# Chunked attention and a two-layer network on one core: first transfers halved, float64 weights decoded with a slope, a gate with one ScalarE pass less, and another issue order

## The chip, the cores and the metric

The kernel runs on one core of a Trainium2 chip. The metric is device time in microseconds of one execution. In the text, PE is TensorE, ACT is ScalarE, DVE is VectorE, and SP is the engine whose queue issues the transfers.

## The reference, cut to what matters

Attention over chunks of 32 queries, each with a window of 64 keys (8 memory keys, 16 left, 32 own, 8 right), and then two matrix products with a piecewise square between them. The two weights of the network come as float64.

```
scores = scale * q_c @ k_full.T                # per chunk: 32 x 64, 4 x 8 heads, 24 chunks
a = exp(scores - max) ; a = a / (sum(a) + 1e-9)
x = a @ v_full                                  # x: 3072 tokens x 512
h = x @ w_in                                    # 512 -> 2048
g = h if h >= 1, 0 if h <= -1, else (h + 1)**2 / 4
out = g @ w_out                                 # 2048 -> 512
```

## The kernel before, in words

The 3072 tokens are six blocks of 512. Each product of the network is made of three products of fp32r parts (high by high, low by high, high by low), so every operand is split on ACT (a copy to fp32r: the high part) and DVE (the difference: the low part). The 2048 hidden features are 16 slices of 128 (`NFC`). For one block and one slice, PE does the first layer (12 matmuls into a bank of `ps_h`, of which there are two), ACT and DVE make the gate from that bank, and PE does the second layer (12 matmuls into the accumulators `a0`, `a1`).

The weights arrive as 16 tiles `w_0` to `w_15` of 1 MB, each with two slices of 128 by 512 float64 in the order of `weight_order`: w_0 holds first-layer slices 0 and 1, w_1 first-layer slice 2 and second-layer slice 0, w_2 first-layer slice 3 and second-layer slice 1, and so on. `decode` makes fp32 words of them: ACT scales the upper words by 2^-112 to move the exponent, DVE shifts the upper word left by 3, ors in the top bits of the lower word, ors in the sign bit, ACT copies the high part, DVE subtracts for the low part.

After the first two blocks the work goes on in a fixed main loop, 64 steps of one block and slice. The first two blocks are the string `FIRST`: an order written out by hand, each name standing for the next piece of one chain of work. Every engine keeps the program order (`InOrder`), so the string sets the queue of each engine:

- `g0` to `g3`: attention of block 0, by halves of the block and of the head pairs (`first_attention`). PE scores, DVE maximum and subtraction, ACT exponential, DVE sum, reciprocal and product, PE transposes, ACT copy `pt`, PE values into `ps_x`, ACT copy `xth`, DVE difference `xtl`. g0 and g1 are tokens 0 to 255, g2 and g3 tokens 256 to 511.
- `w0` to `w15`: `decode` of one tile.
- `A0` to `A3` and `B0` to `B3`: block 0, slices 0 to 3, with the first half of the tokens (A) and the second (B). `J4` to `J15`: slices 4 to 15 with all tokens. Pieces of each: first layer, gate on ACT, gate on DVE, high part, low part, second layer (`early_step`). `C`, `D`, `E`: the same for block 1.
- `n0` to `n3`: attention of blocks 1 and 2. `+`: the next transfer of the list `early`.

A0 to A3 need g0 and g1 complete, B0 to B3 need g2 and g3. In the gate, ACT makes `relu(h/2 + 1/2)`, `relu(h - 1)` and the square of the first, and DVE makes `min(square, 1) + relu(h - 1)`; `ps_h` is free when the second relu is done. All eight banks are taken: two of `ps_h`, and two each under the tags `s`, `a0` and `a1`, where scores and values of `g` and `n` also live. In the main loop `gating(s)` and `gate_sum(s - 1)` do the same.

Of the kernel before, what the change touches and what calls it, by code (L numbers as in the profile page):

```python
# [31 lines left out]
FIRST = """  # L32
    + + g0 g0 + g0 g1 g0 + g0 g1 g1 g0 g0 + g1 g0 w0 g1 g0 + g1 g1 g1 g0 w0 g1 + w0 g2 g1 w0 g1 g2 +
    w0 g2 w1 g0 w0 + g2 w1 g1 g2 + g0 g2 g2 g2 + g0 g2 w1 g3 g2 g1 w1 + A0 w2 g3 w1 g3 A1 w2 + g3 w1
    w3 g3 g2 A0 g3 g3 + A1 g3 A2 w2 g2 w4 g3 g2 A2 A0 w2 g3 A0 + g3 w3 w2 A0 w3 A0 g3 g3 + w2 B0 A1
    w3 A3 A1 B0 + A1 w3 B0 B1 w4 B0 w3 A3 A1 + B1 B0 w4 w5 B2 B1 w6 A2 w4 n0 + A2 B1 A2 w4 B1 A2 A3
    w5 A3 B2 + A3 w5 B3 w8 B2 w7 B0 w4 + B2 w5 B3 A3 w9 B2 B3 B1 w6 B3 + w5 w6 J4 w10 B3 w5 + w6 w11
    B2 w7 J4 w7 J5 + w6 w7 w12 w6 + w7 B3 J4 J5 w8 J6 w7 + J4 J5 w13 J4 w9 J5 J4 J6 w9 + J5 w15 J6
    w9 J7 J6 w14 J6 n0 w9 J5 J7 w9 w8 J7 J8 w8 J7 J7 w8 w11 J6 w8 J8 w11 J8 J9 w10 J8 w10 w11 J7 J9
    J8 w10 w11 J9 n0 w10 J10 J9 w10 n0 J9 w12 J8 J10 w12 w12 J11 J10 w12 w11 J10 J10 w13 J9 J11 w12  # L40
    w13 w14 J12 J11 n0 J11 n0 n0 J10 n0 J12 J11 n0 n0 J13 n0 n0 n0 n0 J11 w13 J13 J12 w13 J13 w14
    J12 n0 J13 w13 J12 J14 + n0 w14 n0 n0 w14 J12 w14 J14 J13 J14 w15 J14 n1 w15 w15 J15 + n1 w15
    w15 J13 J15 n1 J15 n1 J14 C0 J15 n1 J14 n1 n1 C0 n1 n1 J15 C1 n1 n1 J15 n1 C1 n1 n1 C1 C0 C1 C2
    J15 J15 C0 C1 n1 J15 J15 C0 C2 C2 C0 + n1 C2 n1 n1 C3 C2 C1 C3 C3 D0 C3 C3 C2 D0 D0 D1 D0 D0 n2
    D1 D1 D2 D1 + n2 C3 D1 D2 n2 D0 D2 n2 D2 D3 n2 D2 D1 n2 n2 D3 n2 E4 D3 n2 D3 n2 n2 n2 D2 E4 D3
    n2 E5 n2 E4 E4 E4 D3 E5 E6 E5 E5 E5 E4 E6 E6 E6 n2 E6 E7 + n2 n2 n2 E7 n3 E5 + n2 n2 E7 E8 E7 n2
    E7 n2 E6 n2 E8 n2 n3 E8 E9 E8 n3 E8 E7 n3 E9 n3 E9 n3 n3 n3 E10 E9 E9 E8 E10 n3 n3 E10 n3 E11
    E10 E10 n3 E9 E11 n3 n3 E11 E12 E11 E11 E10 n3 + E12 n3 E12 n3 n3 E13 E12 E12 n3 E11 E13 n3 n3
    E13 E14 E13 E13 n3 E12 n3 E14 n3 E14 E15 E14 E14 E13 E15 E15 E15 E15
"""  # L50
# [18 lines left out]
def attn_ffn_kernel(ctx: ExitStack, tc: tile.TileContext, first_qk, first_v, qk, vw, w, out):  # L69
# [32 lines left out]

    def load_first_qk(g):

        if g == 0:
            t = apool.tile([P, 2, 2 * QKN], F32, name="qk0", tag="qk")
            qk_of[0, 0], qk_of[0, 1] = t[:, 0], t[:, 1]
        elif g > 1:
            qk_of[0, g] = const.tile([P, 2 * QKN], F32, name=f"qk0_{g}", tag=f"w_{NPW - 5 + g}")
        sp.dma_start(qk_of[0, g], first_qk[g])  # L110

    def load_first_v(g):
        if g % 2 == 0:
            if g == 0:
# [3 lines left out]
            v_of[0, g], v_of[0, g + 1] = t[:, 0], t[:, 1]  # L118
        sp.dma_start(v_of[0, g], first_v[g])
# [23 lines left out]

    def words(i):
        pairs = raw[i].rearrange("p (n two) -> p n two", two=2)
        return pairs[:, :, 0], pairs[:, :, 1]

    def decode(i):

        low, u = words(i)  # L150
        high = u.bitcast(F32)

        act.activation(high, high, AF.Copy, scale=2.0**-112)
        yield
        f = apool.tile([P, n2], U32, name="f", bufs=2)
# [7 lines left out]
        ws[i] = const.tile([P, 2 * n2], F32R, name=f"wr_{i}", tag=f"w_{i}")  # L163
        hi, lo = ws[i][:, 0:n2], ws[i][:, n2 : 2 * n2]
        act.copy(hi, f)
        yield
        dve.tensor_tensor(lo, f, hi.bitcast(F32), op=ALU.subtract)
        yield
# [44 lines left out]
    def first_attention(g):  # L213
# [264 lines left out]
    def gating(s):  # L478

        h = hidden.pop(s)  # L480
        g = gpool.tile([P, TB], F32, name="gw", tag="gw")
        t = gpool.tile([P, TB], F32, name="gt")
        act.activation(g, h, AF.Relu, bias=0.5, scale=0.5)
        act.activation(t, h, AF.Relu, bias=-1.0)
# [30 lines left out]
    def early_step(name, blk, tokens, fc):  # L515
# [25 lines left out]
        g, t, gh, gl = (x[:, n * HT : n * HT + size] for x in tiles)
# [4 lines left out]
        dve.scalar_tensor_tensor(g, g, 1.0, t, op0=ALU.min, op1=ALU.add)  # L546
        yield
# [38 lines left out]
    def keep_warm(n):  # L586
# [5 lines left out]

    early = [
        (load_first_qk, 0), (load_first_qk, 1), (load_first_v, 0), (load_w, 0), (load_first_v, 1),
        (load_first_qk, 2), (load_w, 1), (load_first_qk, 3), (load_first_v, 2), (load_first_v, 3),
        (load_w, 2), (load_w, 3), (load_w, 4), (load_qk, 1, 0), (load_v, 1, 0),
    ]
    early += [(load_w, i) for i in range(5, NPW)]
    early += [(load, blk, half) for blk, half in ((1, 1), (2, 0), (2, 1), (3, 0)) for load in (load_qk, load_v)]
    early = iter(early)  # L600

# [7 lines left out]
        "n": lambda i: attention((1 + i // 2, i % 2)),  # L609
        "w": decode,  # L610
    }
    parts = {"A": (0, (0, 1)), "B": (0, (2, 3)), "J": (0, range(NT))}
    parts |= {"C": (1, (0, 1)), "D": (1, (2, 3)), "E": (1, range(NT))}
    chains = {}
    for name in FIRST.split():
        if name == "+":
            load, *which = next(early)
            load(*which)
            continue
        if name not in chains:  # L620
# [15 lines left out]
    for s in range(first * NFC, steps):  # L636
# [40 lines left out]
    gate_sum(steps - 1)  # L677
    gate_high(steps - 1)
# [94 lines left out]
```

## Time and profile before

| | |
|---|---|
| median of 3 runs | 595.48 us (595.32 to 595.52) |
| the profiled execution | 595.43 us, of which the span from first to last instruction is 593.7 us |
| mean granted clock of TensorE | 0.985 of full |
| busy share: PE, PEld, DVE, ACT | 97%, 81%, 60%, 49% |
| read from and written to memory | 48.23 MB, 6.29 MB |

The profile's page is one execution. A busy PE can be a PE at half its clock, and matmul ends are modelled. Idle time of an engine costs only where the engine bounds its stretch, so the rows are read by stage: the first 35 us, where the clock falls and PE waits, the stretch to 110 us, and the main loop behind it.

### The profile page before, as it was taken

How to read it: one execution, taken by the hardware profiler on the slowest of the kernel's cores; microseconds unless marked ns; L12 is line 12 of the kernel's file. 1: busy time of each engine (PE TensorE's matmuls, PEld its weight loads, DVE VectorE, ACT ScalarE, POOL GpSimd, SP SyncE). 2: the span in 40 equal slices, each digit the busy share in tenths (PEclk: the TensorE clock that was granted, in tenths of full speed). 3: DMA queues.
4: the chain of work that ended last, by engine and by line, in shares of the span. 5: the costliest groups of instructions: out<-in, count | busy, mean ns of one | idle time of the engine just before them, and what ended most of it. 6: DMA issues, size and time to landing. Idle time of an engine off the chain costs nothing.

```text
span 593.7 us, 12316 instructions
## 1 busy us (share of the span) xinstructions
PE 577.6 (97%) x5496; PEld 478.1 (81%) x5496; DVE 357.6 (60%) x506; ACT 288.9 (49%) x511; POOL 0.7 (0%) x6
## 2 busy tenths in 40 slices
PE   5899999999999999999999999999999999999996
PEld 2788888798888888888888888888888888888885
DVE  5999999986576434756723674833584752322222
ACT  2689864545454444444535353444443453543342
POOL 0000000000000000000000000000000000000000
PEclk8599999999999999999999999999999999999999
DMA  8999300425050203113201223201320000100001
GB/s 353 424 416 421 161 0 1 175 75 182 0 179 1 72 1 139 42 71 108 72 1 72 108 72 108 72 1 39 140 72 2 1 2 0 72 0 2 0 1 71
DMA packets 9845, 55.32 MB, mean 93 GB/s; under 512 B 1088, under 2 KB 1088, under 8 KB 5184
## 3 DMA queue, kind: packets, MB, share of 16 engines
q1 hardware_dynamic: 9792, 54.53, 24.0%
q8 instruction: 43, 0.70, 0.5%
q14 instruction: 10, 0.08, 0.0%
HBM read 48.23 MB, written 6.29 MB: 92 GB/s over the span
## 4 chain that ended last, share of the span: by engine, by line
PE 81%; DVE 15%; issue 2%; DMA 1%; ACT 0%; DVEq 0%; ACTq 0%
PE ps_o L63 39%; PE ps_h L63 38%; DVE f L63 6%; DVE wr L63 2%; PE ps_s L63 2%; PE ps_x L63 2%; DVE gw L63 1%; DVE gl L63 1%; DVE pr L63 1%; DVE den L63 1%; DMA qk<-in_first_qk_dram 1%; DVE pt L63 1%; DVE mx L63 1%; DVE xtl L63 0%; DVE rin L63 0%
## 5 line engine op out<-in xcount | busy, mean ns | idle before, releaser
L63 PE MATMUL ps_h<-xth,wr 128*128 128x512 f32 (+1 forms) x832 | 195.4, 377 | 1.0 <-DVE wr L63 1.0
L63 PE MATMUL ps_o<-wr,gh 128*128 128x512 f32 x768 | 194.6, 390 | 0.0
L63 PEld LDWEIGHTS ps_h<-xth,wr 128*128 128x128 f32 x832 | 148.7, 190 | 30.6 <-DVE wr L63 1.5
L63 PEld LDWEIGHTS ps_o<-wr,gh 128*128 128x128 f32 x768 | 143.3, 188 | 29.4
L63 DVE SCALAR_TENSOR_TENSOR gw<-gw,gt 128x512 f32<-128x512 f32 (+1 forms) x104 | 67.2, 648 | 139.3 <-ACT gw L63 138.8
L63 ACT ACTIVATE gw<-ps_h 128x512 f32<-128x512 f32 (+1 forms) x104 | 58.5, 562 | 152.5 <-PE ps_h L63 152.5
L63 PE MATMUL ps_o<-wr,gl 128*128 128x512 f32 x384 | 106.9, 389 | 0.0
L63 PE MATMUL ps_h<-xtl,wr 128*128 128x512 f32 (+1 forms) x416 | 104.8, 374 | 0.0
L63 ACT CAST gh<-gw 128x512 fp32r<-128x512 f32 (+1 forms) x104 | 60.9, 587 | 72.8 <-DVE gw L63 72.8
L63 DVE TENSOR_TENSOR gl<-gw,gh 128x512 fp32r<-128x512 f32 (+1 forms) x104 | 67.3, 648 | 45.7 <-ACT gh L63 45.5
L63 PEld LDWEIGHTS ps_h<-xtl,wr 128*128 128x128 f32 x416 | 75.3, 190 | 13.9
L63 PEld LDWEIGHTS ps_o<-wr,gl 128*128 128x128 f32 x384 | 72.1, 188 | 15.1
L63 ACT ACTIVATE gw<-gw 128x512 f32<-128x512 f32 (+1 forms) x104 | 62.3, 599 | 0.0
L63 ACT ACTIVATE gt<-ps_h 128x512 f32<-128x512 f32 (+1 forms) x104 | 58.2, 559 | 0.0
L63 DVE STREAM_TRANSPOSE pt<-pr 32x512 f32<-32x512 f32 (+1 forms) x60 | 41.2, 698 | 1.2
L63 DVE SCALAR_TENSOR_TENSOR f<-w,f 128x1024 uint32<-128x1024 uint32 x32 | 38.9, 1220 | 0.4
L63 DVE STREAM_TRANSPOSE xt<-xr 32x512 f32<-32x512 f32 (+1 forms) x48 | 32.9, 699 | 8.8 <-ACT xr L63 8.2
L63 ACT ACTIVATE pr<-pr 128x1024 f32<-128x1024 f32 (+1 forms) x14 | 13.1, 937 | 33.2 <-DVE pr L63 33.0
L63 ACT CAST wr<-f 128x1024 fp32r<-128x1024 f32 x16 | 16.8, 1048 | 11.5 <-DVE f L63 11.5
L63 PEld LDWEIGHTS ps_s<-qk 64*32 64x32 f32 x1536 | 16.9, 110 | 6.2 <-issue 3.1
L63 DVE COPY ob<-ps_o 128x512 f32<-128x512 f32 (+1 forms) x16 | 9.6, 620 | 18.8 <-PE ps_o L63 18.8
L63 PE MATMUL ps_s<-qk 64*32 64x64 f32 x1536 | 19.4, 236 | 1.2 <-DMA qk<-in_first_qk_dram 1.2
(33 smaller groups left out, 216.4 us busy)
## 6 DMA issues: line engine op xcount, KB each, us to landing
w<-in_w_dram SPq DMA_DIRECT2D x16, 1024.0 KB, 19.8
qk<-in_qk_dram SPq DMA_DIRECT2D x10, 1536.0 KB, 6.7
v<-in_vw_dram SPq DMA_DIRECT2D x10, 1024.0 KB, 5.1
out_dram<-ob SPq DMA_DIRECT2D x24, 256.0 KB, 2.0
qk<-in_first_qk_dram SPq DMA_DIRECT2D x4, 768.0 KB, 8.7
v<-in_first_v_dram SPq DMA_DIRECT2D x4, 512.0 KB, 12.7
```

The source lines that it names most:

```text
L63: return self.tc.keep_in_program_order(getattr(self.engine, name)(*args, **kwargs))
```

## The change

Six edits. (1) `first_qk` is loaded in two halves per group, and the parts of w_0 and w_1 in one transfer per slice; the order of transfers is now written into `FIRST` as `L0` to `L39` (index into the list `loads`). (2) In g0 the maximum and the subtraction run by halves (`HALVED`). (3) The four slices of w_0 and w_1 are decoded one by one (`u0` and `u1` are the slices of w_0, `u2` and `u3` those of w_1), from raw tiles that lie in the places of w_10 and w_9. (4) The sign in `decode` comes from a Prelu with slope -2^32 on ACT in place of the scaling copy, and the DVE pass that ored the sign in is gone. (5) The gate is `min(max(h, 1), square)`: ACT's `relu(h - 1)` is gone, and DVE reads h from `ps_h`. (6) `FIRST` is another order. `SUMMED` is empty, so that branch is not taken. For A and B the gate tiles are now keyed by pair.

```diff
 FIRST = """
-    + + g0 g0 + g0 g1 g0 + g0 g1 g1 g0 g0 + g1 g0 w0 g1 g0 + g1 g1 g1 g0 w0 g1 + w0 g2 g1 w0 g1 g2 +
-    w0 g2 w1 g0 w0 + g2 w1 g1 g2 + g0 g2 g2 g2 + g0 g2 w1 g3 g2 g1 w1 + A0 w2 g3 w1 g3 A1 w2 + g3 w1
...
+    L0 L1 g0 g0 g0 g0 L2 g0 L3 L5 g0 L9 L8 L10 L13 L12 L4 L6 g1 g1 u0 g1 g0 L7 g1 g2 u2 u0 g0 g1 L11
+    L14 g0 g1 g0 g1 g0 u0 g1 g2 u0 g0 g1 u0 g2 u2 g2 g3 u2 g2 u1 g3 g0 g2 g3 g2 g1 u1 g0 L16 g3 L15
+    g2 g1 g0 u2 g1 g2 L17 g3 g2 g1 g3 u1 g3 A0 g3 g2 u3 u2 A0 u1 L30 A0 u1 A0 A0 g3 u3 A1 u3 g3 w2
+    g3 A2 w2 u3 L19 A1 g3 g2 w2 u3 A1 A0 w2 w3 g3 A2 g2 B0 n0 L18 w2 A2 B0 w3 A1 L21 L20 L26 L22 w5
...
+    J8 J7 J7 w12 n1 w10 J8 J6 J10 J9 w12 w13 J9 w11 n1 J10 J7 J9 n1 w11 J10 n1 w10 w11 w10 J10 J9 n1
+    w10 J9 J10 J13 J8 J13 n1 J13 J13 J11 w13 w14 C0 n2 w11 w15 J13 C0 J11 n1 n1 n2 w15 C0 J11 J9 w15
...
+SUMMED = ()
+HALVED = (0,)
+SLICED = (0,1)
...
+        at = slice(r * QKN, (r + 1) * QKN)
+        sp.dma_start(qk_of[0, g][:, at], first_qk[g, :, at])
...
-            raw[i] = const.tile([P, 2 * n2], U32, name=f"w_{i}", tag=f"w_{i}")
+            tag = f"w_{NPW - 6 - i}" if i < len(SLICED) else f"w_{i}"
+            raw[i] = const.tile([P, 2 * n2], U32, name=f"w_{i}", tag=tag)
...
-        act.activation(high, high, AF.Copy, scale=2.0**-112)
+        act.activation(high, high, AF.Prelu, scale=2.0**-112, alpha=-(2.0**32))
...
-        dve.scalar_tensor_tensor(f, u, 0x80000000, f, op0=ALU.bitwise_and, op1=ALU.bitwise_or)
-        yield
...
+        for at in (slice(0, 1), slice(1, 2)) if g in HALVED else (slice(0, 2),):
...
+            dve.tensor_reduce(mk, sr, axis=AX.X, op=ALU.max)
...
+                dve.tensor_tensor(mr, sr, mk.unsqueeze(3).to_broadcast([P, 2, 2 * k, W]), op=ALU.subtract)
...
-        act.activation(t, hp, AF.Relu, bias=-1.0)
         act.activation(g, g, AF.Square)
         yield
-        dve.scalar_tensor_tensor(g, g, 1.0, t, op0=ALU.min, op1=ALU.add)
+        dve.scalar_tensor_tensor(g, hp, 1.0, g, op0=ALU.max, op1=ALU.min)
...
+    loads = [
+        (load_first_qk, 0, 0), (load_first_qk, 0, 1), (load_first_qk, 1, 0), (load_first_qk, 1, 1),
+        (load_first_v, 0), (load_w, 0, (0,)), (load_w, 0, (1,)), (load_first_v, 1),
+        (load_first_qk, 2, 0), (load_first_qk, 2, 1), (load_w, 1, (0,)), (load_w, 1, (1,)),
+        (load_first_qk, 3, 0), (load_first_qk, 3, 1), (load_first_v, 2), (load_first_v, 3),
+    ]
+    loads += [(load_w, i) for i in range(2, NPW)]
```

The main loop's `gating` and `gate_sum` (now `gate_least`) change in the same way as the gate above. The order of each queue that the text speaks of, read off the new string:

- SP: L0 to L3 (qk of g0, g1), L5 (slice 0 of w_0), L9, L8 (qk of g2), L10 (first slice of w_1), L13, L12 (qk of g3), L4 (v of g0), L6 (second slice of w_0), L7 (v of g1), L11 (second slice of w_1), L14 (v of g2), L16 (w_2), L15 (v of g3), L17 (w_3), L30 (qk of n0) and on.
- PE: scores of g0, g1, g2; transposes of g0, g1; scores of g3; values of g0, g1; transposes of g2; first layer of A0; values of g2; transposes of g3; first layer of A1; values of g3; first layer of A2; second layer of A0; first layer of B0; scores of n0; and on, to first layers of J10, J9, second of J7, first of J13.
- DVE: g0, g1 to their products, with a piece of u0 between; maximum of g2, low part of u0, subtraction of g2, two pieces of u2, sum of g2, maximum of g3, subtraction of g3, product of g2, `xtl` of g0, sum of g3, `xtl` of g1, the or of u1, product of g3, low part of u2, gate of A0, and on.
- ACT: exponential of g2, slope of u1, `pt` of g1, `xth` of g0, exponential of g3, high part of u2, `xth` of g1, `pt` of g2, slope of u3, gate of A0, and on.

## Rows read from the trace of the kernel before

**Rows 1.** The page's first part: busy time of an engine, share of the span, number of instructions.
```profile
PE 577.6 (97%) x5496; PEld 478.1 (81%) x5496; DVE 357.6 (60%) x506; ACT 288.9 (49%) x511; POOL 0.7 (0%) x6
```

**Rows 2.** Who PE waited for, over the whole run: us in total, times, longest.
```profile
PE ps_h L63 <- DVE pr L63: 6.8, 3, 4.2
PE ps_h L63 <- DVE wr L63: 1.0, 1, 1.0
```

**Rows 3.** Busy time of the engines by stretch: start and end, length, busy us (instructions) of PE, PEld, DVE, ACT and POOL, then the granted clock, the share of the transfer engines, GB/s.
```profile
9.00:10.00 1.00, 0.00 (x0) 0.00 (x0) 0.97 (x3) 0.00 (x0) 0.00 (x0) 0.83 0.95 397
26.00:27.00 1.00, 1.00 (x8) 1.00 (x7) 1.00 (x3) 1.00 (x2) 0.00 (x0) 0.63 1.07 434
34.00:60.00 26.00, 26.00 (x269) 22.75 (x265) 25.90 (x36) 23.02 (x43) 0.00 (x0) 1.00 1.01 419
60.00:105.00 45.00, 45.00 (x319) 37.32 (x317) 44.48 (x56) 28.02 (x45) 0.00 (x0) 1.00 0.11 48
```

**Rows 4.** PE in order of time: start, length, what; in brackets the idle time before and what ended it.
```profile
5.03 1.18 PE L63 MATMUL ps_s<-qk 64*32 64x64 f32 x64 [0.25 <-DMA qk<-in_first_qk_dram]
6.91 0.86 PE L63 MATMUL ps_s<-qk 64*32 64x64 f32 x64 [0.70 <-DMA qk<-in_first_qk_dram]
...
16.18 3.64 PE L63 MATMUL ps_x<-pt,v 64*64 64x32 f32 x128
...
23.95 2.07 PE L63 MATMUL ps_h<-xth,wr 128*128 128x256 f32 x8
...
31.22 0.60 PE L63 MATMUL ps_h<-ident,pr 128*128 128x128 f32 x4
...
32.93 1.13 PE L63 MATMUL ps_x<-pt,v 64*64 64x32 f32 x64 [1.11 <-ACT pt L63]
33.99 1.19 PE L63 MATMUL ps_o<-wr,gh 128*128 128x512 f32 x4
...
36.91 1.12 PE L63 MATMUL ps_h<-xth,wr 128*128 128x256 f32 x8
...
39.79 1.09 PE L63 MATMUL ps_o<-wr,gh 128*128 128x512 f32 x4
...
41.18 1.11 PE L63 MATMUL ps_h<-xth,wr 128*128 128x256 f32 x8
...
64.75 1.98 PE L63 MATMUL ps_h<-xth,wr 128*128 128x512 f32 x8
...
67.47 1.98 PE L63 MATMUL ps_o<-wr,gh 128*128 128x512 f32 x8
```

**Rows 5.** Groups of instructions by form over the whole run: busy us, mean ns of one, idle time before them and what ended most of it.
```profile
L63 DVE SCALAR_TENSOR_TENSOR gw<-gw,gt 128x512 f32<-128x512 f32 x88 | 60.6, 690 | 135.0 <-ACT gw L63 134.5
L63 ACT ACTIVATE gt<-ps_h 128x512 f32<-128x512 f32 x88 | 52.1, 592 | 0.0
L63 DVE SCALAR_TENSOR_TENSOR f<-w,f 128x1024 uint32<-128x1024 uint32 x32 | 38.9, 1220 | 0.4
L63 DVE TENSOR_TENSOR pr<-ps_s,mx 128x512 f32<-128x512 f32 x4 | 2.8, 691 | 0.1
L63 ACT ACT_TABLE_LOAD x1 | 1.3, 1283 | 0.7 <-PEq L759 0.7
```

**Rows 6.** DVE in order of time (columns as in rows 4), and one row of ACT. From start to start of neighbours one reads what an instruction costs when the next does not wait for it.
```profile
6.29 0.11 DVE L63 MEMSET ps_s<- 32x64 f32 x1 [5.16 <-PE ps_s L63]
...
7.88 0.63 ACT L63 ACTIVATE pr<-pr 128x512 f32<-128x512 f32 x1 [5.87 <-DVE pr L63]
...
38.23 0.41 DVE L63 TENSOR_TENSOR gl<-gw,gh 128x256 fp32r<-128x256 f32 x1
38.56 0.41 DVE L63 SCALAR_TENSOR_TENSOR gw<-gw,gt 128x256 f32<-128x256 f32 x1
...
53.60 1.22 DVE L63 SCALAR_TENSOR_TENSOR f<-w,f 128x1024 uint32<-128x1024 uint32 x1
54.74 0.69 DVE L63 TENSOR_SCALAR f<-w 128x1024 uint32<-128x1024 uint32 x1
...
59.00 0.68 DVE L63 SCALAR_TENSOR_TENSOR gw<-gw,gt 128x512 f32<-128x512 f32 x1
59.60 0.69 DVE L63 TENSOR_SCALAR f<-w 128x1024 uint32<-128x1024 uint32 x1
```

**Rows 7.** Transfers of the first 5 us: first SP's queue in order of time (start, length, what), then, from the list of issues, size and us from issue to landing of three of them (qk of g2, w_1, qk of g3).
```profile
3.29 0.49 SPq L63 DMA_DIRECT2D qk<-in_first_qk_dram  x1
3.81 0.45 SPq L63 DMA_DIRECT2D w<-in_w_dram  x1
4.30 0.45 SPq L63 DMA_DIRECT2D qk<-in_first_qk_dram  x1
...
qk<-in_first_qk_dram SPq DMA_DIRECT2D x1, 768.0 KB, 11.7
w<-in_w_dram SPq DMA_DIRECT2D x1, 1024.0 KB, 13.7
qk<-in_first_qk_dram SPq DMA_DIRECT2D x1, 768.0 KB, 15.1
```

**Rows 8.** One step of the main loop in order of time: the latest gate on DVE in the steps around 250 us, and the first layer that takes the same bank next.
```profile
249.86 0.69 DVE L63 SCALAR_TENSOR_TENSOR gw<-gw,gt 128x512 f32<-128x512 f32 x1
...
256.84 1.98 PE L63 MATMUL ps_h<-xth,wr 128*128 128x512 f32 x8
```

More of the change, by code (lines that the diff above doesn't have):

```diff
@@ L38 @@
[L38 to L47, printed above, removed]
@@ L142, in weights, with decode @@
         return ws[i][:, c0 : c0 + DM]
[L144 to L150, printed above, removed]
+    def decode(i, parts=(0, 1)):
+        at = slice(parts[0] * DM, (parts[-1] + 1) * DM)
+        pairs = raw[i].rearrange("p (n two) -> p n two", two=2)[:, at]
+        low, u = pairs[:, :, 0], pairs[:, :, 1]
         high = u.bitcast(F32)
-        act.activation(high, high, AF.Copy, scale=2.0**-112)
+        act.activation(high, high, AF.Prelu, scale=2.0**-112, alpha=-(2.0**32))
         yield
-        f = apool.tile([P, n2], U32, name="f", bufs=2)
+        f = apool.tile([P, n2], U32, name="f", bufs=2)[:, at]
         dve.tensor_scalar(f, u, 3, None, op0=ALU.logical_shift_left)
@@ L159, in decode @@
         yield
-        dve.scalar_tensor_tensor(f, u, 0x80000000, f, op0=ALU.bitwise_and, op1=ALU.bitwise_or)
-        yield
         f = f.bitcast(F32)
-        ws[i] = const.tile([P, 2 * n2], F32R, name=f"wr_{i}", tag=f"w_{i}")
-        hi, lo = ws[i][:, 0:n2], ws[i][:, n2 : 2 * n2]
+        if i not in ws:
+            ws[i] = const.tile([P, 2 * n2], F32R, name=f"wr_{i}", tag=f"w_{i}")
+        hi, lo = ws[i][:, 0:n2][:, at], ws[i][:, n2 : 2 * n2][:, at]
         act.copy(hi, f)
@@ L196, in normalise, with divide @@
     def normalise(pr):
-        n = pr.shape[1]
-        den = apool.tile([P, n], F32, name="den", bufs=2)
+        den = apool.tile([P, pr.shape[1]], F32, name="den", bufs=2)
         dve.tensor_reduce(den, pr, axis=AX.X, op=ALU.add)
         yield
+        yield from divide(pr, den)
+    def divide(pr, den):
+        n = pr.shape[1]
         dve.tensor_scalar_add(den, den, 1e-9)
@@ L478, in gating, with gate_least @@
     def gating(s):
[L480 to L484, printed above, removed]
-        act.activation(g, g, AF.Square)
-        gate[s] = (g, t)
-    def gate_sum(s):
-        g, t = gate[s]
-        dve.scalar_tensor_tensor(g, g, 1.0, t, op0=ALU.min, op1=ALU.add)
-        gate[s] = g
+        g = gate[s] = gpool.tile([P, TB], F32, name="gw", tag="gw")
+        act.activation(g, hidden[s], AF.Relu, bias=0.5, scale=0.5)
+        act.activation(g, g, AF.Square)
+    def gate_least(s):
+        g = gate[s]
+        dve.scalar_tensor_tensor(g, hidden.pop(s), 1.0, g, op0=ALU.max, op1=ALU.min)
     def gate_high(s):
@@ L519, in early_step @@
         xh, xl = (x[:, :, tokens[0] * P : tokens[0] * P + size] for x in xts[blk])
-        n = 0
+        n, key = 0, ("g", name)
         if size < TB:
-            n = len(halves) % 2
+            pair, n = divmod(len(halves), 2)
+            key = ("g", pair)
             halves.append(name)
@@ L529, in early_step @@
         yield
-        if n == 0:
-            tiles = (
+        if key not in both:
+            both[key] = (
                 gpool.tile([P, TB], F32, name="gw", tag="gw"),
-                gpool.tile([P, TB], F32, name="gt"),
                 gpool.tile([P, TB], F32R, name="gh", bufs=3),
@@ L590, in keep_warm, with start_load @@
             pe.matmul(ps, warm[:, 0:P], warm, start=True, stop=True)
[L593 to L596, printed above, removed]
-    ]
-    early += [(load_w, i) for i in range(5, NPW)]
-    early += [(load, blk, half) for blk, half in ((1, 1), (2, 0), (2, 1), (3, 0)) for load in (load_qk, load_v)]
-    early = iter(early)
+    loads = [
[3 more added lines that the diff above has]
+        (load_first_qk, 3, 0), (load_first_qk, 3, 1), (load_first_v, 2), (load_first_v, 3),
+    ]
+    loads += [(load_w, i) for i in range(2, NPW)]
+    loads += [(load, blk, half) for blk, half in ((1, 0), (1, 1), (2, 0), (2, 1), (3, 0)) for load in (load_qk, load_v)]
+    def start_load(i):
+        load, *which = loads[i]
+        load(*which)
+        yield
     gpool.tile([P, 32], F32, name="offset", bufs=1)
@@ L610, in attn_ffn_kernel @@
         "w": decode,
+        "u": lambda i: decode(i // 2, (i % 2,)),
+        "L": start_load,
     }
@@ L615, in attn_ffn_kernel @@
     for name in FIRST.split():
[L616 to L619, printed above, removed]
         if name not in chains:
@@ L647, in attn_ffn_kernel @@
         if s > first * NFC:
-            gate_sum(s - 1)
+            gate_least(s - 1)
             gate_high(s - 1)
@@ L676, in attn_ffn_kernel @@
                     pass
-    gate_sum(steps - 1)
+    gate_least(steps - 1)
     gate_high(steps - 1)
```

87 lines of the change are left out of this document (56 added, 31 removed).

## The prediction, made before the changed kernel was run

> **What bounds the kernel now.** I read PE's busy share first, then who PE waits for, then the stretches, then the timeline of the first 40 us. PE is busy 97% [rows 1]. Its waits inside the span are few: transposes of the first groups for a DVE product, and one wait of 1.0 for a decoded weight [rows 2]. From 34 to 105 us PE is full at full clock, and DVE is full beside it [rows 3]. So the change can win only where PE loses time now: ahead of 34 us, and in that one wait.
>
> How much is lost there? I price PE's work at full clock: scores of one g 0.86, four transposes 0.60, values of one g 1.13, a half first layer 1.44 (two of them from 36.91 to 39.79), a half second layer 1.39, a whole layer 2.72 [rows 4]. When the first second layer starts at 33.99, PE has done four scores, four transposes, four values and three half first layers: 3.44 + 2.40 + 4.52 + 4.32 = 14.7. So 19.3 of the first 34.0 us are lost, part of it because the granted clock stood at 0.5 (1.2 GHz) from about 9.7 to 26.7 [rows 3]: A0's first eight matmuls took 2.07 against 1.12 [rows 4]. With the wait of 1.0 the loss is 20.3. The number and shapes of the matmuls don't change, so the new time is the old one, less 20.3, plus the loss under the new order.
>
> **The change part by part.** *The sign.* DVE loses one pass per decoded tile, 16 x 1.22 = 19.5 us [rows 5], of a queue that is full until 105. The slope on ACT is not in the trace. Below it costs nothing more than the scaling copy it replaces; above, one table load of 1.28 [rows 5] whenever ACT turns between exponential and slope. The trace loads one table for exponential, relu, square and copy together, so I take nothing, and keep the load for a rival.
>
> *The gate.* ACT loses 592 ns of each whole step [rows 5], off the path now. DVE's pass reads h from PSUM: a subtraction from PSUM takes 691 ns, the old gate from SBUF alone 690 [rows 5], so nothing for the pass. But `ps_h` is held until DVE has read it. In the main loop the latest gate I see ends at 250.55, and the next first layer in that bank starts at 256.84 [rows 8]: 6.3 us of cover, nothing on the path. In the first stretch it counts, below.
>
> *Halved transfers and maximum.* Half of 768 KB lands sooner, but PE's warm-up matmuls run until about 4.8, against a start of the scores at 5.03 [rows 4]: 0.2. The half maximum could start before the other half's scores. Against that, the mask of 32 rows, written by the first part of the scores of either half, started at 6.29, just behind the last score (5.03 + 1.18) [rows 4, 6]; so the first maximum waits for all. Two passes of 256 in place of one of 512 then cost 2 x 0.33 against 0.60 [rows 6], twice, plus one more hand-over. The exponential of g0 comes at 7.8, as now (7.88, rows 6): I take nothing. If the halves do start apart, 0.6 at most.
>
> *Order of transfers.* Each landing I place by the KB ahead of it. In the trace, with 4352, 5376 and 6144 KB, landings are 15.0, 17.5 and 19.4 [rows 7] (issue plus latency). In the new order v of g0 is behind 4608 KB with its own (15.6), slice 1 of w_0 behind 5120 (16.9), v of g1 behind 5632 (18.1). These are later than now, while the qk of g2 and g3 come earlier: DVE does the softmaxes first.
>
> *The order, walked through.* DVE's instructions cost, from start to start, 1.14 at 1024 elements, 0.60 at 512 or for the shift of a tile, 0.33 at 256 [rows 6]; where one waits for the one before, 0.1 more. I walk DVE's queue as the front lists it:
> - g0 and g1 are done with their products at 12.0 and 13.4 (g1's maximum no longer stands behind g0's sum).
> - Maximum of g2 to 14.0, low part of u0 to 14.6, subtraction of g2 to 15.2. Now PE may write g3's scores over g2's: at half clock 15.4 to 16.6 (as 1.18 at 5.03, and a little more).
> - Values of g0 (v at 15.6): 128 matmuls for two groups took 3.64 at half clock [rows 4], so 1.8 each: 16.6 to 18.4. Values of g1 need v (18.1) and `pt`, which on ACT stands behind the slope of u1, and so behind slice 1 of w_0 (16.9): `pt` at 18.0. 18.4 to 20.2.
> - Transposes of g2 (its product is done at 19.3) 20.2 to 21.3. First layer of A0 from 21.3; `xtl` of g1 is there at 21.6, before its last four matmuls. At half clock 2 x 1.44: to 24.2. Now A0 starts at 23.95 [rows 4].
>
> By 24.2 PE has done four scores, three transposes, two values and one half layer: 3.44 + 1.80 + 2.26 + 1.44 = 8.9. Loss 15.2. From there PE's next needs are met with 0.1 to 2 us to spare (u3 decoded at 30.1 for A0's second layer, asked for at 30.3; gate of A3 at 38.5 for B2's bank, asked for at 38.5) up to the first layer of J13, which needs a bank freed by the gate of J10 or J9. PE's work until then is one transpose group, two values, seven half first and eight half second layers, eleven whole layers, and two scores and one values of n at twice g's: 0.6 + 2.3 + 10.1 + 11.1 + 29.9 + 5.7 = 59.7, so PE is there at 83.9. DVE's queue from the or of u1 (21.7) through the gate of J10 is 88 instructions: 26 at 1024 (29.6), 11 shifts (6.6), 22 at 512 (13.2), 17 at 256 (5.6), six 32-row transposes of 512 (4.3 at the 0.7 of a 512 pass run alone), eight small ones (1.3): 60.6, so 82.3, plus about 1.9 of waits (for A0's gate, for the slopes of w_2 and A2 on ACT): 84.2. The two meet. If the bank is J9's, nothing is lost; at worst 1.6 (DVE's 84.2 against PE's rows for n, which can be shorter than twice g's). I take 0.8. Behind it the same walk gives PE 1 to 4 us of slack on each decoded tile, and the wait of 1.0 is gone.
>
> **Sum.** New loss 15.2 + 0.8 = 16.0, against 20.3: 4.3 less. The profiled execution was 595.43 (span 593.7 and 1.7 around it), the median 595.48, so they may stand for each other: 595.4 - 4.3 = **591.1**. Its bounds: 1.0 less for a clock that is back before A0's first layer (1.4) or halves that start apart (0.6), 0.8 for the bank either way, and hand-overs of 0.05 to 0.1 over the twenty joints of the walk (up to 2 more): 589 to 593.
>
> **The rivals.**
> *The clock returns early* or never falls: PE now stands idle from 7.8 to 12.0, in the new order it has g2's scores at 10 to 11. Then A0 ends 2.7 sooner (1.3 of earlier values and transposes, 1.4 of the layer itself), if DVE keeps up, which it doesn't fully: 588.0 to 589.
>
> *Table switches on ACT.* If the slope isn't in the table of the exponential, the new queue of ACT has 12 turns between the two, seven by the slope of u3, each 1.28 [rows 5]. At least two (around u0, between the exponentials of g0 and g1) fall on DVE's chain, 2.6; at most all seven, 9.0. With three, the third before u3 and w_2, 3.9: 595.0, about no change; the bounds are 593.7 and 600. For it: no row has this function. Against it: one load served four functions.
> The Trainium skill, ScalarE: Activation LUTs, section Table sets: the hidden batching unit, says that functions are loaded as named sets and that turning to another set costs a load; its list names relu, copy and abs as in every set and doesn't name Prelu. By its figure of about 2.7 us a switch, three would cost 8.0 and the time would be about 599.
>
> *Slow small transfers, late values.* The price on the other side: A0 needs v of g1, behind 5632 KB in pieces of 384 and 512 KB. With the loss at 16.0, it becomes slower than now once v of g1 lands 4.3 later, at 22.4 or after. From the first group's landing at 5.0, 4864 KB (4.98 MB) remain, so this decides below 286 GB/s. At 260 GB/s it lands at 24.2: 597. Against it: at 9 to 10 us, with five of the eight transfers in flight at 512 or 768 KB, the rate was 397 GB/s, against 419 later with 1024 KB each [rows 3].
> The Trainium skill, DMA: Bandwidth & Descriptors, section Bandwidth, has the rule to batch transfers to 1 MiB or more for 75% of the peak; at 75% of the 419 the values would land at 20.9, and the time would be 593.9. This trace speaks against the rule for transfers of half a MiB; for 384 KB no run here shows it yet.
>
> *The bank held by DVE in the main loop.* If 64 steps lost 0.1 each, 6.4: 597.5. It decides where the gate ends more than 6.3 us later than at 250.55 [rows 8].
>
> *The gain moves on.* The order is tight, and a later wait for DVE takes it back: 595. DVE's queue of 60.6 would have to be 7% longer.
>
> **How the numbers follow.** Forecast 0.70; clock 0.08; table switches 0.10 (spread 593.7 to 597: faster 0.02, same 0.05, slower 0.03); late values 0.05; bank in the main loop 0.03; gain moves on 0.04. A measurement of this kernel tells about 0.2% (1.2 us) from no change. Faster 0.70 + 0.08 + 0.02 = 0.80; same 0.05 + 0.04 = 0.09; slower 0.03 + 0.05 + 0.03 = 0.11. Range 588.0 to 594.5: from the early clock to the lower part of the switches; left out are most of the switches and the last three rivals, a little under 0.2.
>
> **What would show it.** Right: first layer of A0 near 21.3, PE's waits behind 25 us under 2 in all, one table load, DVE's sign pass gone, 16 x 1.22 less in the groups, no PE waits behind 120. Wrong: A0 behind 23, or more than one table load, or PE waits for DVE's gate between 25 and 110 of more than 3.

## The result, and the profile after

The changed kernel takes 599.54 us (median of 4 runs, 598.39 to 599.84) against 595.40 for the kernel before on the same chip: a ratio of 1.0066, 95% interval 1.0053 to 1.0078. It is slower by 4.1 us where 4.3 less was forecast; 591.1 is missed by 8.4. The profiled span is 597.8.

The first part of the page of the changed kernel answers [rows 1]:

```profile
PE 579.1 (97%) x5496; PEld 479.4 (80%) x5496; DVE 338.8 (57%) x498; ACT 252.3 (42%) x411; POOL 0.7 (0%) x6
```

Groups by form over the whole run (columns as in [rows 5]): the tables that ScalarE loads, the gate on VectorE, and the slope of a whole tile on ScalarE:

```profile
L69 ACT ACT_TABLE_LOAD x1 | 1.3, 1283 | 0.7 <-PEq L787 0.7
...
L69 DVE SCALAR_TENSOR_TENSOR gw<-ps_h,gw 128x512 f32<-128x512 f32 x88 | 60.6, 689 | 133.9 <-ACT gw L69 133.4
...
L69 ACT ACTIVATE w<-w 128x1024 f32<-128x1024 f32 x14 | 15.9, 1159 | 0.0
```

The operations did what they were costed at: VectorE is busy 18.8 us less, ScalarE 36.6 less, there is one table load, and the gate from PSUM takes 689 ns as the old one took 690. PE has the same number of matmuls. So the loss lies in what PE waits for. Who PE waited for, over the whole run (answers [rows 2]):

```profile
PE ps_s L69 <- DMA qk<-in_first_qk_dram: 6.4, 3, 5.3
PE ps_h L69 <- issue: 2.6, 1, 2.6
PE ps_x L69 <- issue: 2.2, 1, 2.2
PE ps_h L69 <- DVE warm L69: 1.2, 1, 1.2
PE ps_s L69 <- DVE pr L69: 0.8, 1, 0.8
PE ps_h L69 <- DVE gw L69: 0.5, 1, 0.5
PE ps_s L69 <- issue: 0.3, 1, 0.3
```

The waits for VectorE's products are down from 6.8 [rows 2] to 0.8, and the wait for a decoded weight is gone. In their place stand a longer wait for the transfers of qk (6.4, where the kernel before had 1.2), and two pauses, of 2.6 and 2.2, that are put down to "issue": PE waited for nothing that the trace shows. PE in order of time (columns as in [rows 4]) has their places:

```profile
12.74 1.18 PE L69 MATMUL ps_s<-qk 64*32 64x64 f32 x64 [5.27 <-DMA qk<-in_first_qk_dram]
...
16.61 1.19 PE L69 MATMUL ps_s<-qk 64*32 64x64 f32 x64 [0.78 <-DVE pr L69]
17.72 2.69 PE L69 MATMUL ps_x<-pt,v 64*64 64x32 f32 x77
22.65 1.70 PE L69 MATMUL ps_x<-pt,v 64*64 64x32 f32 x51 [2.24 <-issue]
...
25.05 2.05 PE L69 MATMUL ps_h<-xth,wr 128*128 128x256 f32 x8
...
39.23 0.52 PE L69 MATMUL ps_h<-xtl,wr 128*128 128x256 f32 x3
42.32 0.37 PE L69 MATMUL ps_h<-xtl,wr 128*128 128x256 f32 x1 [2.57 <-issue]
42.49 1.91 PE L69 MATMUL ps_h<-xth,wr 128*128 128x256 f32 x8
```

Both pauses cut a row of like matmuls in two: the values of g0 and g1 behind the 77th of 128, and the first layer of A3 behind the 11th of 12. No data can be late for the 78th that was there for the 77th of the same tiles. Behind the second pause the clock stands at 1.2 GHz (granted 0.50 from 42 to 45 us): the first eight matmuls of B1 take 1.91 where they take 1.12 at full clock [rows 4].

### The profile page after: what moved, and what is told of

Same layout as the page of the kernel before. It is cut to its first block, busy times and chain, and to the rows that moved or that the text cites. A ratio compares the mean times of both kernels' runs of the same rounds, so it can differ in the third digit from the quotient of the medians.

```text
span 597.8 us, 12247 instructions
## 1 busy us (share of the span) xinstructions
PE 579.1 (97%) x5496; PEld 479.4 (80%) x5496; DVE 338.8 (57%) x498; ACT 252.3 (42%) x411; POOL 0.7 (0%) x6
## 4 chain that ended last, share of the span: by engine, by line
PE 89%; DVE 5%; issue 2%; DMA 2%; ACT 1%; SPq 0%; DVEq 0%; ACTq 0%
PE ps_h L69 42%; PE ps_o L69 41%; PE ps_x L69 3%; PE ps_s L69 3%; DVE f L69 2%; DMA qk<-in_first_qk_dram 2%; DVE wr L69 1%; DVE gl L69 1%; DVE gw L69 1%; ACT gw L69 1%; DVE pt L69 0%; SPq L69 0%; DVE den L69 0%; DVE mx L69 0%; ACT w L69 0%
## 5 line engine op out<-in xcount | busy, mean ns | idle before, releaser
L69 DVE SCALAR_TENSOR_TENSOR gw<-ps_h,gw 128x512 f32<-128x512 f32 (+1 forms) x104 | 67.2, 647 | 139.7 <-ACT gw L69 139.1
L69 PEld LDWEIGHTS ps_s<-qk 64*32 64x32 f32 x1536 | 16.4, 108 | 12.2 <-DMA qk<-in_first_qk_dram 7.7
L69 ACT CAST wr<-f 128x1024 fp32r<-128x1024 f32 (+1 forms) x18 | 17.1, 951 | 10.5 <-DVE f L69 10.5
L69 ACT ACTIVATE w<-w 128x1024 f32<-128x1024 f32 (+1 forms) x18 | 18.6, 1051 | 5.8 <-DMA w<-in_w_dram 5.8
L69 DVE TENSOR_TENSOR wr<-f,wr 128x1024 fp32r<-128x1024 f32 (+1 forms) x18 | 19.8, 1100 | 1.8 <-ACT wr L69 1.7
## 6 DMA issues: line engine op xcount, KB each, us to landing
v<-in_first_v_dram SPq DMA_DIRECT2D x4, 512.0 KB, 10.8
```

What stands on the lines that cost most here:

```text
L69: return self.tc.keep_in_program_order(getattr(self.engine, name)(*args, **kwargs))
```

## The experiments

**The theory formed from this.** PE's instructions come in blocks of 256. PE holds the block that it works in and the next one, and the block after that is asked for when PE enters the next. Where PE issues 256 instructions in less time than a fetch takes, it pauses, at a place that the count of instructions sets. The page's row of the instruction queue gives the size: the changed kernel has 2 x 5496 = 10,992 instructions on PE (each matmul and each weight load is one), 42.9 times 256, and the row below has 43 packets. Attention runs through a block fastest: the scores of one g are 64 matmul instructions with 64 weight loads, and take 0.86 to 1.2 us. The rivals are something that the two stretches wait for but the trace doesn't name (a transfer, a bank), or a VectorE queue that is simply too tight.

```profile
q8 instruction: 43, 0.70, 0.5%
```

The Trainium skill, Runtime: NRT & Kernel Launch, section Instruction fetch mechanics, describes such blocks (16 KiB, 256 instructions, fetched over a queue of the engine's own while the current block runs) and calls the cost of crossing a boundary mostly hidden. The number of packets agrees; that it is hidden, the rows above and the runs below contradict.

**Moving the boundaries.** 64 instructions more ahead of everything should move the pauses by 32 matmuls and leave the work behind them alone; in the kernel before, whose one pause is 0.20 long, they should make a long one.

```
-    keep_warm(8)
+    keep_warm(6)                    # and behind it, in keep_warm:
+        for i in range(34):
+            q = slice(32 * (i % 4), 32 * (i % 4) + 32)
+            pe.matmul(ps[q, 0:32], warm[q, 0:32], warm[q, 0:32], start=True, stop=True)
```

The changed kernel with them (shift64):

> The changed kernel with 64 more PE instructions ahead of the first scores (two of the eight warm-up matmuls become 34 of 32x32); nothing else differs. Theory 1, PE runs out of instructions: they come in blocks of 256, and a block takes 5 to 6 us while the transfer engines are full. Then the two pauses move 32 matmuls earlier in the program: none at matmul 13 of the values of g1 nor at the last one of A3's first layer; instead up to 0.5 us near matmul 45 of the values of g0 and up to 1 us near matmul 107 to 111 of the scores of n0, the clock stays up, and the time is 595 us (593 to 597). Theory 2, the pauses are late data (values, decoded weights): they stay at the same matmuls and the time stays at 599.5 (within 0.7).

The kernel before with them (before_shift64):

> The kernel before with 64 more PE instructions ahead of the first scores, as in shift64; nothing else differs. Theory 1 (instruction blocks): the block that PE entered at the first values now begins at the end of the scores of g2 (15.9 us), and the next is wanted near matmul 45 of the values of g0 (17.4 us) but comes 5 to 6 us after that entry: a pause of 3.5 to 4.5 us there, part of it in time in which PE waited for DVE anyway: 597.5 us (596.5 to 600). Theory 2 (late data): 595.4, unchanged.

PE in order of time, first the changed kernel shifted, then the kernel before shifted:

```profile
18.21 1.49 PE L69 MATMUL ps_x<-pt,v 64*64 64x32 f32 x45
19.94 2.55 PE L69 MATMUL ps_x<-pt,v 64*64 64x32 f32 x83 [0.24 <-issue]
...
33.53 0.40 PE L69 MATMUL ps_h<-xtl,wr 128*128 128x256 f32 x2 [1.72 <-issue]
...
36.66 1.30 PE L69 MATMUL ps_s<-qk 64*32 64x64 f32 x107
39.72 0.42 PE L69 MATMUL ps_s<-qk 64*32 64x64 f32 x21 [1.75 <-issue]
```

```profile
16.27 3.20 PE L63 MATMUL ps_x<-pt,v 64*64 64x32 f32 x110
21.57 0.84 PE L63 MATMUL ps_x<-pt,v 64*64 64x32 f32 x18 [2.10 <-issue]
```

The first pause went from the 77th to the 45th matmul, 32 earlier to the instruction, and shrank, because the block before it is now entered 2.7 us earlier. The second went from the layer of A3 into the scores of n0, and a new one of 1.72 stands in the layer of A2. The kernel before, with nothing changed but its warm-up, got a pause of 2.10 and went to 597.49 us, ratio 1.0036 (1.0023 to 1.0049). I had expected it near the 45th value matmul and 3.5 to 4.5 us long; it stands behind the 110th, 128 matmuls after the place where I had the block begin, so I had counted the block too short. No data and no order was touched, so the count of instructions sets the place of a pause. The time of the shifted new kernel, 598.7 (596.39 to 602.31; the rows are from an execution of 597.08), ratio 1.0055 (1.0037 to 1.0072), is above the 593 to 597 that I expected, since three pauses of 3.7 together took the place of two of 4.8.

**The price of a block by itself.** Behind the last layer come small matmul instructions with nothing loaded, then more of them with the 16 tiles of w loaded again. Each form ran once. A first form, 1536 and 2048 of them, put all matmuls on the same rows and columns:

> The changed kernel with more work behind its last layer, for the cost of the blocks by itself: 768 small matmuls of the scores' shape (64 x 32, 64 columns) while nothing is loaded, then the 16 slices of w loaded once more (16 MB) with 1024 such matmuls beside them. Theory (blocks of 256 instructions, that is 128 matmuls with their weight loads, of which PE holds the one it works in and the next): groups of 128 matmuls with pauses between them; a group takes the time of a fetch, about 2.0 us without transfers and 5.3 to 7 us with them, so 12 and 40 us in all. Rival (the pauses have to do with what the matmuls wait for, not with their number): both run through at about 13.5 ns each, 10.4 and 13.8 us.

One took 56 ns there, later 107, so 128 of them took 7 us or more, longer than a fetch, and no pause shows; that run tells nothing of the time of a block. Its count fits: 7168 added instructions are 28 blocks, and its instruction queue has 71 packets, 28 more than the changed kernel. The second form, 1024 and 1024, lays them out as the scores do:

> The changed kernel with more work behind its last layer, as the run before it in this row, but the small matmuls now lie as the scores do (both halves of the rows, four groups of columns, two banks), so that one takes 13.5 ns as there: 1024 of them with their weight loads, 2048 instructions, with nothing loaded, then as many beside 16 MB of loads. Theory (blocks of 256, one fetched at a time): without transfers 8 blocks of about 2 us, near 16 us; with them 8 blocks of 5.3 to 8 us, 42 to 64 us. Rival (PE doesn't wait for its instructions): 14 us both times.

```
+    def small(n):
+        for i in range(n):
+            s = two_banks("s", "ps_s").rearrange("p h (t w) -> p h t w", w=D)
+            ...                     # 32 matmuls of ident on itself, placed as in pe_scores
+    small(16)
+    sp.dma_start(ident, first_qk[0, :, 0:P])
+    for i in range(NPW):
+        t = const.tile([P, 2 * n2], U32, name=f"again_{i}", tag=f"w_{i}")
+        sp.dma_start(t, w[i].bitcast(U32))
+    small(16)
```

PE in order of time, without transfers and from 622.63 on with them, and the row of the instruction queue:

```profile
598.42 2.48 PE L69 MATMUL ps_s<-ident 64*32 64x64 f32 x128 [1.73 <-issue]
601.88 2.85 PE L69 MATMUL ps_s<-ident 64*32 64x64 f32 x128 [0.97 <-issue]
605.33 2.85 PE L69 MATMUL ps_s<-ident 64*32 64x64 f32 x128 [0.60 <-issue]
...
619.70 0.90 PE L69 MATMUL ps_s<-ident 64*32 64x64 f32 x40 [0.88 <-issue]
622.63 1.88 PE L69 MATMUL ps_s<-ident 64*32 64x64 f32 x87 [2.03 <-DMA ident<-in_first_qk_dram]
628.66 2.85 PE L69 MATMUL ps_s<-ident 64*32 64x64 f32 x128 [4.15 <-issue]
634.58 2.85 PE L69 MATMUL ps_s<-ident 64*32 64x64 f32 x128 [3.08 <-issue]
640.77 2.85 PE L69 MATMUL ps_s<-ident 64*32 64x64 f32 x128 [3.35 <-issue]
647.24 2.85 PE L69 MATMUL ps_s<-ident 64*32 64x64 f32 x128 [3.62 <-issue]
```

```profile
q8 instruction: 58, 0.95, 0.6%
```

From the first pause on, each stands 128 matmul instructions behind the one before, that is 256 with the weight loads (of the 88 from 622.63 on the trace has 87). They stand 24 matmuls into a tile's 64 (the first stands behind 216, that is 3 x 64 + 24), so the change of a bank is not the cause. Before the tail PE had long matmuls and time to fetch ahead; it still ran through only 216, the 88 that were left of its block and the 128 of the next, so it held no more than these. From one block to the next it takes 3.45 us without transfers (3.73 at the end) and 5.9 to 6.5 with them. The 3.45 is the same whether the 128 matmuls take 2.48 or 2.85, as it should be if a fetch begins when PE enters a block. One block does not fit: it was entered at 619.70, ahead of the loads, and the next came at 628.66, 9.0 us later; why is open. The 4096 added instructions are 16 blocks, and the queue has 15 packets more. The rival (no waiting for instructions) is out; my 2 us for a block without transfers was too low for this place. The changed kernel has a block at 102 us, with few loads, that came in about 2.2 (n2's scores start at 101.87; by count the block was entered some three matmuls ahead of them, and a pause of 0.31 stands ahead of 103.63).

**Taking the pauses out of the new order.** n0's scores are 128 matmul instructions and as many weight loads, a whole block in 1.5 us. They, with n0's maximum and subtraction, go behind the first layer of B2:

```
-    ... g2 B0 n0 L18 w2 ... L31 n0 A3 w3 ... L32 B0 B2 B2 n0 n0 B3 B2 w4 w5 n0 ...
+    ... g2 B0 L18 w2 ... L31 A3 w3 ... L32 B0 B2 n0 B2 B3 B2 n0 n0 n0 w4 w5 n0 ...
```

With 40 instructions more in front (n0_later: `keep_warm(7)` and 21 of the small matmuls), and then with the 64 of above (shift64_later):

> The changed kernel with two edits that take no work out: 40 more PE instructions ahead of the first scores (7 large warm-up matmuls and 21 small ones), and n0's 128 score matmuls, its maximum and subtraction four PE steps later, behind the first layer of B2. Theory (PE's instructions arrive in blocks of 256, and the block after the one entered takes 5.3 to 7 us while the loads run): no stretch from 13 to 45 us asks for 256 instructions in less than that, so the pauses of 2.24 and 2.57 shrink to under 1 together, the clock doesn't fall behind 30 us, and of the 4.8 + 1.8 that they cost about 6 comes back: 593.6 (592.5 to 594.5), faster than before. Rival (the order is too tight for DVE, and the pauses only show it, or the gain moves on): the time stays at 597 or above, with waits for DVE in place of the pauses.

> The changed kernel with both of the edits that moved one pause each: 64 more PE instructions ahead of the first scores, and n0's scores behind the first layer of B2. What is asked: is the new order faster than before once PE doesn't pause for its instructions? If the pauses are what the prediction lacked: about 0.2 is left of the pause in the values, some of the 1.7 in A2's first layer, none in n0's scores; with 1 us of waits for VectorE moved in, as in the run with n0's scores later, the span is 595.3 - 1.75 + 1 = 594.5, the time 594.5 to 596.5, no slower than before, and not the 591.1 either, since the scores of g2 still come 3 us behind the forecast. Rival (VectorE's tight queue takes back what PE gains): 597.4 or more, as with 40 instructions.

n0_later took 597.38 us, ratio 1.0034 (1.0023 to 1.0045), not the 593.6 expected. The second pause was gone, the first was not: 2.53 behind the 57th value matmul, 8 us after the block before was entered, by count. Shifted by 64 the pauses are down to 1.07 and 0.79, and the time is 596.0 us, ratio 1.0013 (1.0004 to 1.0023), as expected. Who PE waited for in that last kernel:

```profile
PE ps_s L69 <- DMA qk<-in_first_qk_dram: 6.2, 3, 4.8
PE ps_h L69 <- DVE warm L69: 1.2, 1, 1.2
PE ps_o L69 <- DVE gl L69: 1.1, 1, 1.1
PE ps_x L69 <- issue: 1.1, 1, 1.1
PE ps_h L69 <- DVE gw L69: 0.8, 2, 0.7
PE ps_h L69 <- issue: 0.8, 1, 0.8
```

So these two edits brought back 3.5 of the 8.4 us (3.2 by the ratios), and 1.9 us of pauses are left. The rest did not come back: PE, now earlier, waits 1.1 and 0.8 for VectorE. Without most of its pauses the new order stands 0.8 us behind the kernel before, not ahead of it.

**Why the transfers were late.** From 5 to 10 us the changed kernel moved 329 GB/s, the kernel before 418. The suspects are the halves of qk, the halves of w_0 and w_1, and the order. The runs: first qk alone whole, then w_0 and w_1 too, both in the new order; last the kernel before with only w_0 and w_1 in halves.

```
whole_qk and whole_all
-        at = slice(r * QKN, (r + 1) * QKN)
-        sp.dma_start(qk_of[0, g][:, at], first_qk[g, :, at])
+        if (g, "whole") not in both:
+            both[g, "whole"] = True
+            sp.dma_start(qk_of[0, g], first_qk[g])
whole_all
-        a, b = parts[0] * n2, (parts[-1] + 1) * n2
+        if parts == (1,):
+            return
+        a, b = 0, 2 * n2
before_half_w
-        a, b = parts[0] * n2, (parts[-1] + 1) * n2
-        sp.dma_start(raw[i][:, a:b], w[i, :, a // 2 : b // 2].bitcast(U32))
+        for half in ((0,), (1,)) if i < 2 and len(parts) == 2 else (parts,):
+            a, b = half[0] * n2, (half[-1] + 1) * n2
+            sp.dma_start(raw[i][:, a:b], w[i, :, a // 2 : b // 2].bitcast(U32))
```

> The changed kernel with qk of g0 to g3 loaded whole (four transfers of 768 KB, at the place of the first half of each) in place of eight halves. Theory A, halved rows move slower: the rate at 6 to 10 us is back at 400 GB/s or more from about 310, scores of g2 start at 10 to 11.5 us in place of 12.7, A0 starts about 1 us earlier and the time is 598.3 us (597.5 to 599). Theory B, the rate has another cause: still under 350 GB/s at 7 to 9 us, no change of the time beyond 0.7.

> The changed kernel with qk of each group, w_0 and w_1 loaded in one transfer each, as in the kernel before, the order of the loads kept. Theory (the halves are why only 329 GB/s move from 5 to 10 us, against 418 before): 400 GB/s or more from 5 to 10, g2's scores at 10.3 to 10.8. Rival (the order of the loads, or the number of them that the queue holds, sets the rate): 270 to 350 GB/s from 6 to 9 us as with qk alone whole, g2's scores at 11 or later. The time itself stays near 599 in both, 598 to 600, since the two pauses of PE for instructions lie behind it.

> The kernel before with w_0 and w_1 loaded in two transfers of half the columns each, nothing else changed. Theory (half slices move slowly): from 5 to 10 us 330 to 370 GB/s in place of 418, the values and the first layer 0.5 to 1.5 later, 596 to 597. Rival (the halves move as fast as the whole): 418 GB/s within 15, and the time within 0.3 of 595.3.

The stretch from 5 to 10 us (columns as in [rows 3]) of the kernel before, the changed kernel, whole_qk, whole_all and before_half_w, in this order:

```profile
5.00:10.00 5.00, 2.04 (x128) 1.64 (x128) 2.92 (x6) 0.63 (x1) 0.00 (x0) 0.97 1.01 418
```
```profile
5.00:10.00 5.00, 1.30 (x96) 0.81 (x96) 3.92 (x10) 1.44 (x3) 0.00 (x0) 1.00 1.02 329
```
```profile
5.00:10.00 5.00, 1.98 (x128) 1.58 (x128) 3.63 (x9) 1.66 (x3) 0.00 (x0) 0.98 0.95 349
```
```profile
5.00:10.00 5.00, 1.92 (x128) 1.60 (x128) 3.64 (x9) 1.24 (x3) 0.00 (x0) 0.91 1.01 421
```
```profile
5.00:10.00 5.00, 1.94 (x128) 1.61 (x128) 2.97 (x6) 0.63 (x1) 0.00 (x0) 0.93 0.93 340
```

The halves of w are the main cause: making them whole too takes the new order from 349 to 421, and halving them alone takes the old order from 418 to 340, and from 595.33 to 596.1 us, ratio 1.0014 (1.0005 to 1.0024). The transfer engines did not idle in the changed kernel: their share is 1.02 at 329 GB/s. Size alone can't be it: the 512 KB of v, with rows of 4 KB like those of a half, moved among the transfers at 418 in the kernel before. What sets a half apart is that its rows lie apart in memory; that was not tried by itself. The times were 599.56 for whole_qk, ratio 1.0075 (1.0058 to 1.0092), and 600.64 for whole_all, ratio 1.009 (1.0072 to 1.0108). I had g2's scores of whole_all at 10.3 to 10.8 and they came at 12.59: I forgot that the second half of w_0, now in the same transfer as the first, goes ahead of them. Its two pauses are 3.38 and 2.72 in place of 2.24 and 2.57; the first block took as long as in the changed kernel (5.9 against 5.8 us from its asking), but the values ran mostly at full clock up to it.

**One operation of the change at a time.** The runs are the slope alone in the old order (slope_old_order, with the steps of the removed pass taken out of `FIRST`), the old gate in the new one (old_gate: the gate's lines of the diff ahead of the prediction, reversed), and the old sign pass in the new one (old_sign). The gate alone in the old order wasn't tried: I judged that a bank would be held there for VectorE past the point where PE needs it, which no run shows.

slope_old_order, and in reverse old_sign (the pass there in the step of the or):

```
-        act.activation(high, high, AF.Copy, scale=2.0**-112)
+        act.activation(high, high, AF.Prelu, scale=2.0**-112, alpha=-(2.0**32))
-        dve.scalar_tensor_tensor(f, u, 0x80000000, f, op0=ALU.bitwise_and, op1=ALU.bitwise_or)
```

> The kernel before with one part of the change alone: the sign by the slope on ACT, the DVE pass that ored it in removed, its tokens taken out of the order; gate, order and transfers as before. If the slope costs what the scaling copy cost, DVE is 19.5 us shorter, the wait of 1.0 at 107 us is gone and A0 starts 1 to 2 us earlier: 593.5 us (592.5 to 594.5). If PE's instruction blocks bound the head, the 1 to 2 us are not to be had and only the wait of 1.0 goes: 594.4. One table load in both.

> The changed kernel with the gate of before (two relus and a square on ScalarE, then the minimum plus the second relu on VectorE, from SBUF), all else as changed. If the gate is worth nothing in time, as the prediction costed it: 599.5 within 1.0, with the two pauses at the same matmuls. If ScalarE's 592 ns per step are on the path of the new order: 601 or more, with longer waits of PE for the gate between 30 and 110 us.

> The changed kernel with the sign of before (a scaling copy on ScalarE and a fourth pass of 1.22 us per tile on VectorE), all else as changed. If VectorE's queue is full until 105 us, as the prediction has it, 16 x 1.22 = 19.5 us more of it, less the 4 to 7 us that PE's pauses give VectorE to catch up, come back as waits of PE: 608 to 615. If the pauses hide what the pass costs: 600 to 603.

slope_old_order took 594.05 us, ratio 0.9986 (0.9976 to 0.9995), with the wait of 1.0 for a weight gone: a gain of 1.2 by the medians and of 0.3 to 1.4 by the interval, the best that one edit gave. old_gate took 598.98, ratio 1.006 (1.0044 to 1.0077), no different from the changed kernel: the gate is worth nothing that these runs can tell, as costed. Its second pause stands one matmul later and is put down to ScalarE's `gh`, which had ended half a microsecond before. old_sign took 615.95, ratio 1.0348 (1.0332 to 1.0363): in the new order the sixteen passes cost 16.4 us of their 19.5, nearly all. The same passes cost 1.2 in the old order. So the new order needs nearly all of what the slope saves on VectorE.

**The clock.** 14 large matmuls of the warm-up kind in PE's idle time from 8 to 12 us of slope_old_order:

```
-    + + g0 g0 + g0 g1 g0 + g0 ...
+    + + g0 g0 + g0 g1 K0 g0 + g0 ...          # K0: keep_warm(14)
```

> The kernel before with the slope in place of the sign pass (594.05 in its own run), and 14 large warm-up matmuls on PE behind g1's scores, where it stands idle from 8 to 12 us, to keep the clock at 2.4 GHz. If the clock alone holds the head back: values 2.3 in place of 3.6, first layers of A0 and A1 1.45 in place of 2.9 and 2.1, 591 to 592. If PE's instructions, fetched in blocks, bound the head: the values run ahead of the block that they need and pause 2 to 3.6 us (at the end of the values of g0, 14 matmuls earlier than a count without them), 593 to 595.

The run took 593.9 us, ratio 0.9976 (0.9966 to 0.9985), the lowest time of this study, though its interval overlaps that of slope_old_order. The clock stayed at 2.4 GHz to about 15.8 (granted 0.99 from 12 to 16) and was at 1.2 in the values all the same (granted 0.50 from 16 to 24), which took 3.57. So the first expectation did not come, and what a kept clock would bring stays open. For the second there is a candidate, the wait ahead of the transposes of g2; first slope_old_order, then this run:

```profile
21.17 1.08 PE L63 MATMUL ps_h<-ident,pr 128*128 128x128 f32 x4 [1.53 <-DVE pr L63]
```
```profile
21.92 1.09 PE L63 MATMUL ps_h<-ident,pr 128*128 128x128 f32 x4 [2.60 <-DVE xtl L63]
```

By count a block now ends close to this place, and it was entered near 15.8. The product that the transposes read ended at 21.02 and 21.09, so they start 0.15 behind it in the one and 0.83 in the other. The trace puts the longer wait down to `xtl`, but in slope_old_order the transposes started ahead of the end of the same `xtl`. So about 0.7 of this wait is likely a block that came some 6 us after the one before was entered, most of it hidden behind VectorE, and the time lies in the 593 to 595 of that expectation; this is argued from the count, not shown.

## Why the prediction was wrong

**Right.** The slope costs what the copy did (16 passes less on VectorE, one table load in all, as before); the gate costs nothing and no wait of PE stands behind 120 us; the halves start apart by nothing that lasts (the exponential of g0 at 7.40, forecast 7.8); VectorE's queue is nearly full from 60 to 105 us (43.25 of 45); J13's bank costs 0.5, forecast 0.8. Late values of g1 didn't decide: v of g1 landed at 19.7, before the 22.4 named.

**Wrong, the first step:** "The number and shapes of the matmuls don't change, so the new time is the old one, less 20.3, plus the loss under the new order." The walk lets PE start a matmul as soon as its data and bank are there. It has no term for the arrival of the instructions themselves, and so puts it at nothing. The new order puts g3's scores directly ahead of the values of g0 and g1, 384 instructions in 4.8 us at half clock, so 256 in 3.2 where a block took 5.8, and n0's scores among half layers. The old order had waits for VectorE between such rows, 6.8 us in all [rows 2], in which blocks could come in; that this is why it hardly paused is argued from the count. Its trace has one pause, in the values of g2:

```profile
29.32 0.43 PE L63 MATMUL ps_x<-pt,v 64*64 64x32 f32 x16 [0.20 <-issue]
```

64 instructions more made one of 2.10 there, in the values of g0 and g1. By the forecast's own steps, the values ran from 17.72 to 24.3 in place of 16.6 to 20.2, and A0 started at 25.05 in place of 21.3, behind the 23 that was named as a sign of being wrong. Of that 3.75 the pause is 2.24, the values around it 0.75, and most of the rest the late scores of g3 (below). The second pause adds 2.57, the half clock behind it 1.2 (from 42.32 to 46.01, 3.7 us for B1's first layer, 1.44 at full clock, and five more matmuls, 1.06).

**Wrong, a size:** the landings. I placed them by KB at the old rate and took the 397 GB/s of one microsecond as evidence for small transfers; the halves of w were not among them. The scores of g2 came at 12.74, forecast near 10; g3's scores came 1.2 late (16.61 for 15.4). VectorE was busy with g0 and g1 to 13.2 anyway, then waited 0.8 for the scores of g2, and after their maximum 0.4 for ScalarE's high part of u0, a wait that the walk did not have. The Trainium skill, DMA: Bandwidth & Descriptors, section Bandwidth, has the rule that speaks for 1 MiB and more. The runs with halves of w side with the rule, 340 against 418 GB/s; the whole transfers of v and qk, of 512 and 768 KB within the 418, do not. I had weighed the price of slow transfers down by the row of 397.

**The sum.** 3.75 for A0, 2.57, 1.2, and J13 with the pause of 0.31 as forecast: 7.5 of 8.4. 0.9 isn't assigned; 0.1 of it is a slip in the forecast, where 24.2 - 8.9 is 15.3 and not 15.2.

**The rival that came nearest** was the tight order, "a later wait for DVE takes it back", at 0.04. It was not the cause, but it is part of what remains when most of the pauses go (the waits of 1.1 and 0.8 for VectorE in shift64_later).

## What to carry to other kernels

Count instructions as well as microseconds: where an order packs small matmuls together, check that any 256 instructions of the engine (weight loads included) last longer than one block takes, here 2.2 to 3.7 us with few or no transfers and mostly 5.4 to 8 with loads running. An "issue" wait that splits a row of like instructions can be such a block (in old_gate one was put down to another engine), and adding a few instructions ahead tells it apart, since it moves by exactly as many. Removing waits of the matrix engine can remove the time in which its instructions arrived.

## What was not expected of the hardware

PE's instructions came in blocks of 256, and from entering one block to having the next it took 5.4 to 8 us while the loads ran (9.0 once) and 3.45 to 3.73 in the tail with nothing loaded. Transfers of half a tile of w, with rows 4 KB long and 4 KB between them, moved 340 GB/s in a stretch where whole tiles gave 418. Two kernels that differ by 64 instructions that compute nothing differ by 2 us.
